# Block-sparse attention and a squared-ReLU MLP on one core: the static value products as one 128-wide stationary operand instead of two of 64

## The chip, the core and the metric

The kernel runs on one core of a Trainium2 chip. A core has a matrix engine (TensorE, PE in the profile) with its own row for loading the stationary operand (PEld), a vector engine (DVE), an activation engine (ACT), a general engine (POOL) and a queue for DMA issues (SP). Matrix products take a stationary operand, which is loaded into the array first, and a moving operand, which then streams past it; the result goes to PSUM banks, everything else lies in SBUF. The metric is the device time of one execution in microseconds (us); the time before is the median of three runs.

## The reference

The attention has 4 batches, 8 heads, 768 positions and 64 values per head. Every block of 32 queries sees its neighbours, the first and the last block, and three sampled blocks; the first and last block of queries see all. The MLP follows on 3072 tokens, with 512 inputs and 2048 hidden units.

```python
mask = |blk_i - blk_j| <= 1, or blk_i or blk_j first or last, or kb in sampled_blocks[qb]
scores = where(mask, q @ k.T / sqrt(64), -1e9)
attn = softmax(scores)
x = attn @ v                               # (4, 8, 768, 64) -> (3072, 512)
h = x @ w_in                               # (3072, 2048)
g = s * relu(h) ** 2 + b
out = g @ w_out                            # (3072, 512), float32
```

## The kernel before, in words

The work has two stages. First comes the attention. It is cut into 52 slots: 40 slots of kind `s` (128 interior queries, four heads each), 4 of kind `h` and 8 of kind `d` for the first and last blocks of queries. For an `s` slot the matrix engine does, in this order: the transposes of the softmax numerators of the slot (`t<-ident,ptile`, line 787; three chunks of 128 keys for each of four heads), the transposes of the result of the slot before (`xs<-ident,xss`, line 858), the scores of the slot after next against its 256 static keys (line 710, or line 724 for the other kinds) and against its sampled keys (line 736), and then the value products of this slot: `av_static` over the two chunks of 128 static keys (line 832) and `av_sampled` over the 96 sampled keys (line 846). Between these, DVE takes the row maxima (line 751), ACT the exponentials (line 763), and both evacuate the transposes to the tiles `pt` (lines 791 and 793). The second stage is the MLP, in products of float32 split into a high and a low part (lines 401 to 403 and 440 to 442), whose last half is done by a seven-product scheme (line 1193).

The order on each engine in the attention and the first part of the MLP is not written by hand: a planner (`Plan.order`) takes operations with costs and priorities and issues each when it could start. One call of `av_static` is one operation of cost 260 in that plan, and that number is the same in both kernels. The matrix engine's own order inside the attention is a fixed line, slot after slot.

`xs` is a PSUM bank of 128 partitions, one per query; `pt[:, c, :]` has 128 keys in its partitions and 128 queries in its columns, and is the stationary operand; `vt[:, c, hp * D:(hp + 1) * D]` has the same keys and the 64 values of one head, and is the moving operand. `halves` are the two slices 0 to 63 and 64 to 127 (of the queries here). The four heads of a slot (`j`) times two chunks (`c`) times two halves make 16 products. The profile counts a float32 product as two records of the stationary load and two of the product, so a slot has 32 of each. A transpose is one record.

Of the kernel before, what the change touches and what calls it, by code (L numbers as in the profile page):

```python
# [202 lines left out]
def kernel(  # L203
# [16 lines left out]
    nc = tc.nc  # L220
# [3 lines left out]
    D = 64  # L224
# [234 lines left out]
    with ExitStack() as es:  # L459
# [240 lines left out]
        halves = [slice(par * D, (par + 1) * D) for par in range(2)]  # L700
# [101 lines left out]
        def out_of(i, j):  # L802
            if i not in xs_of:
                o = bank(NBANK, f"xs{i}")
                nu = 2 if slots[i][0] == "d" else 4
                xs_of[i] = o[:, :nu * D].rearrange("p (h d) -> p h d", h=nu)
                tr_of[i] = o[:, 2 * P:2 * P + nu * D].rearrange("p (a q) -> p a q", q=P)
            return xs_of[i][:, j, :]
# [3 lines left out]
        def av_static(i, j):  # L812
            kind, b, t, x = slots[i]
            n = unit_of[i]
            xs = out_of(i, j)
            if kind == "d":
                vt, pt = vst[(i, j)], pts_of.pop(n + j)
                for c in range(NCH):
                    for par in range(2):
                        rows = halves[par]  # L820
                        nc.tensor.matmul(xs[rows], pt[c // 3][:, c % 3, rows], vt[:, c, rows], start=(c == 0), stop=(c == NCH - 1))  # L821
                return
            vt, pt = vst[(i, 0)], pts_of[n + j][0]
            if kind == "h":
                for par in range(2):
                    nc.tensor.matmul(xs[halves[par]], pt[:, 1, halves[par]], vt[:, (2 * j + par) * D:(2 * j + par + 1) * D],
                                     start=(j == 0), stop=False, skip_group_check=True)
                return
            hp = 2 * (j % 2) + j // 2
            for c in range(2):  # L830
                for rows in halves:
                    nc.tensor.matmul(xs[rows], pt[:, c, rows], vt[:, c, hp * D:(hp + 1) * D], start=(j == 0 and c == 0),  # L832
                                     stop=False, skip_group_check=True)

        def av_sampled(i):
            kind, b, t, x = slots[i]
# [121 lines left out]
        for i, (kind, b, t, x) in enumerate(slots):  # L958
# [52 lines left out]
            for j in range(nu):  # L1011
                pr = j if kind == "d" else 0
                o = op("p", cost[3], u, lambda i=i, j=j: av_static(i, j), cols=col[3], deps=[*evs[j], lv[pr]],
                       alloc=[] if j else [("o", i)], use=[("v", (i, pr)), *(("pt", (u + j, g)) for g in range(ng))] + ([("o", i)] if j else []))
                a_ops.append(o)
# [368 lines left out]
```

## Time and profile before

| | us |
|---|---|
| median of three runs | 809.02 (808.52 to 810.49) |
| profiled execution, its own time | 807.75 |
| span of the instructions in it | 805.9 |
| PE busy in the span | 785.6 (97%) |
| PEld busy | 681.6 (85%) |
| DVE busy | 565.8 (70%) |
| ACT busy | 492.8 (61%) |
| line 832, products, busy | 46.3 (1280 records) |

The profiled execution is 1.27 us below the median. A record of a product reaches from its start to its modelled end, and consecutive records overlap, so the distance between two starts tells more than the length of one. In the timeline a row gives the start, the time from the first start to the last end, the engine and line, the tiles as out<-in, the part of the array as rows*columns, the shape of the operand, and the number of records. In the rows of groups, the numbers behind the bar are busy time and the mean length of one record in ns.

### The profile page before, as it was taken

Reading aid. Unit: us, or ns where it says so; the run is one execution under the profiler, and the core shown is the slowest. Engines: PE = TensorE matmul, PEld = TensorE weight load, DVE = VectorE, ACT = ScalarE, POOL = GpSimd, SP = SyncE. Lnnn points to the kernel's source line nnn. Section 1 sums busy time; section 2 is a strip of 40 time slices with the busy share of each in tenths; the row PEclk is TensorE's granted clock in tenths of the full one; section 3 lists DMA queues with packets and bytes.
Section 4 is the critical chain, followed back from the end, with each engine's and each line's share of the span. In section 5 each row is a group of like instructions: output and inputs, shape, how many; then the busy total and the mean of one; then the engine's idle time right before and its main releaser. Section 6 shows DMA issues by size and latency. Waiting matters only on the chain.

```text
span 805.9 us, 21894 instructions
## 1 busy us (share of the span) xinstructions
PE 785.6 (97%) x8400; PEld 681.6 (85%) x8400; DVE 565.8 (70%) x1445; ACT 492.8 (61%) x1175; POOL 140.9 (17%) x372
## 2 busy tenths in 40 slices
PE   7899998999999999999999999999999999999997
PEld 5588886888887889999899999998889988999996
DVE  5577776888887998999743333388768769766662
ACT  3577776787887787777763333457445457544542
POOL 5422142222400000000000000002223222322321
PEclk8899999999999999999999999999999999999999
DMA  9999798876777533334221010412200012000002
GB/s 252 248 228 325 223 255 247 242 213 206 210 211 248 145 107 108 107 125 131 86 99 39 27 40 27 149 45 88 86 1 7 0 40 90 10 0 1 1 1 78
DMA packets 86071, 95.60 MB, mean 119 GB/s; under 512 B 11344, under 2 KB 64976, under 8 KB 85968
## 3 DMA queue, kind: packets, MB, share of 16 engines
q1 hardware_dynamic: 85968, 94.21, 39.0%
q8 instruction: 66, 1.08, 0.6%
q14 instruction: 37, 0.30, 0.1%
HBM read 77.41 MB, written 12.58 MB: 112 GB/s over the span
## 4 chain that ended last, share of the span: by engine, by line
PE 87%; DVE 5%; DMA 4%; ACT 2%; SPq 1%; issue 1%; DVEq 0%; ACTq 0%
PE m L1193 14%; PE o L441 10%; PE o L442 10%; PE o L440 10%; PE t L787 9%; PE s L710 5%; PE xs L832 5%; PE h L403 5%; PE h L401 5%; PE h L402 5%; PE xs L846 3%; PE s L736 3%; DMA kt<-in_k_seq_dram 2%; PE s L724 1%; PE xs L858 1%; PE xs L821 1%
## 5 line engine op out<-in xcount | busy, mean ns | idle before, releaser
L419 POOL TENSOR_TENSOR hid<-hid,hid 128x384 fp32r<-128x384 f32 x64 | 68.9, 1077 | 512.5 <-ACT hid L1211 510.4
L763 ACT ACTIVATE ptile<-ptile,nm 128x352 f32<-128x352 f32 (+2 forms) x208 | 121.1, 584 | 35.8 <-DVE nm L751 35.5
L1210 ACT ACTIVATE hid<-hid,sb_b,sb_s 128x384 f32<-128x384 f32 x64 | 45.4, 709 | 110.6 <-DVE hid L1204 110.6
L751 DVE CUSTOM_DVE_ANT_0 ptile<-s,ms 128x352 f32<-128x352 f32 x160 | 74.3, 521 | 30.1 <-PE s L736 29.9
L670 POOL COPY kg<-kt 128x128 f32 x264 | 63.9, 302 | 135.1 <-PE s L736 122.6
L401 PE MATMUL h<-x,win 128*128 128x384 f32 x256 | 86.4, 337 | 0.0
L403 PE MATMUL h<-x,win 128*128 128x384 f32 x256 | 86.3, 337 | 0.0
L402 PE MATMUL h<-x,win 128*128 128x384 f32 x256 | 85.9, 336 | 0.0
L787 PE MATMUL t<-ident,ptile 128*128 128x128 f32 x608 | 80.2, 281 | 1.8 <-ACT ptile L763 1.3
L410 DVE SCALAR_TENSOR_TENSOR hid<-hid,sb_s 128x384 f32<-128x384 f32 x64 | 39.4, 616 | 53.9 <-ACT hid L406 53.7
L441 PE MATMUL o<-wout,hid 128*128 128x512 f32 x192 | 76.0, 396 | 0.6 <-DVE wout L85 0.6
L442 PE MATMUL o<-woutr,hid 128*128 128x512 f32 x192 | 75.9, 395 | 0.0
L442 PE MATMUL o<-wout,hid 128*128 128x512 f32 x192 | 75.9, 395 | 0.0
L441 PE MATMUL o<-woutr,hid 128*128 128x512 f32 x192 | 75.8, 395 | 0.0
L440 PE MATMUL o<-wout,hid 128*128 128x512 f32 x192 | 74.8, 390 | 0.0
L440 PE MATMUL o<-woutr,hid 128*128 128x512 f32 x192 | 74.6, 389 | 0.0
L787 PEld LDWEIGHTS t<-ident,ptile 128*128 128x128 f32 x608 | 66.6, 142 | 8.7 <-issue 2.2
L406 ACT ACTIVATE hid<-h 128x384 f32<-128x384 f32 x64 | 31.4, 491 | 69.6 <-PE h L403 69.1
L791 DVE COPY pt<-t 128x384 f32<-128x384 f32 (+1 forms) x104 | 56.3, 543 | 8.3 <-PE t L787 6.6
L419 DVE TENSOR_TENSOR hid<-hid,hid 128x384 fp32r<-128x384 f32 x64 | 35.6, 556 | 34.3 <-ACT hid L415 34.1
L1193 PE MATMUL m<-xT,wop 128*128 128x384 f32 x288 | 58.5, 337 | 0.7 <-DVE sum L1286 0.7
L793 ACT COPY pt<-t 128x384 f32<-128x384 f32 (+1 forms) x104 | 48.1, 474 | 15.3 <-PE t L787 15.2
(169 smaller groups left out, 1660.1 us busy)
## 6 DMA issues: line engine op xcount, KB each, us to landing
vg<-in_v_dram SPq DMA_DIRECT2D x136, 128.0 KB, 3.6
v<-in_v_sta_dram SPq DMA_DIRECT2D x40, 256.0 KB, 4.2
kt<-in_k_seq_dram SPq DMA_DIRECT2D x16, 544.0 KB, 8.0
raw_i<-in_w_in_dram SPq DMA_DIRECT2D x16, 512.0 KB, 4.4
raw_o<-in_w_out_dram SPq DMA_DIRECT2D x16, 512.0 KB, 3.2
v<-in_v_dram SPq DMA_DIRECT2D x16, 384.0 KB, 5.0
xd<-xst SPq DMA_DIRECT2D x44, 128.0 KB, 3.7
out_dram<-ob SPq DMA_DIRECT2D x20, 256.0 KB, 2.4
```

The source lines that it names most:

```text
L401: nc.tensor.matmul(ph, wh, xh, start=(c == 0), stop=False)
L402: nc.tensor.matmul(ph, wh, xl, start=False, stop=False)
L403: nc.tensor.matmul(ph, wl, xh, start=False, stop=(c == NCC - 1))
L419: (eng or nc.vector).tensor_tensor(out=htile(5 + i % 3), in0=t, in1=gh.bitcast(F32), op=ALU.subtract)
L440: nc.tensor.matmul(acc, gh[:, tsl], wout(f, 0), start=first, stop=False)
L441: nc.tensor.matmul(acc, gh[:, tsl], wout(f, 1), start=False, stop=False)
L442: nc.tensor.matmul(acc, gl[:, tsl], wout(f, 0), start=False, stop=last)
L670: nc.gpsimd.tensor_copy(kg[:, m], kts[b][:, :, bass.ds(box["js"][m], BLK)])
L751: nc.vector.tensor_tensor_reduce(out=pt[:, :w], in0=sps.pop((n, g))[:, :w], in1=msk, scale=-scale, scalar=FMAX if g == 0 else nm[:, 0:1], ...
L763: nc.scalar.activation(pt[:, :w], pt[:, :w], AF.Exp, bias=nms[n][:, last:last + 1], scale=-1.0, accum_out=dns[i][:, g, j:j + 1])
L787: nc.tensor.transpose(tp[:, c, :], src[:, c * P:(c + 1) * P], ident)
L1193: nc.tensor.matmul(to, w_, x_, start=(c == 0 and k == 0), stop=(c == 1 and k == 2))
```

## The change

The loop over the two halves of the queries goes. One product takes all 128 columns of `pt` as its stationary operand and writes all 128 partitions of `xs`. The products, the flags of accumulation, the moving operand and the result stay; a slot of kind `s` has eight products instead of sixteen. The other kinds of slot keep their halves.

```diff
             hp = 2 * (j % 2) + j // 2
             for c in range(2):
-                for rows in halves:
-                    nc.tensor.matmul(xs[rows], pt[:, c, rows], vt[:, c, hp * D:(hp + 1) * D], start=(j == 0 and c == 0),
-                                     stop=False, skip_group_check=True)
+                nc.tensor.matmul(xs, pt[:, c, :], vt[:, c, hp * D:(hp + 1) * D], start=(j == 0 and c == 0), stop=False, skip_group_check=True)
```

The matrix engine's order of one `s` slot before, from the last sampled scores to the first sampled value product; the shape is that of the output, and x4 is two chunks times two halves of one head:

```order
L736 MATMUL s_1512<-kg_1_651,qr_1s 32x96 x4
L832 MATMUL xs_1537<-v_0_1031,pt_0_1492 64x64 x4
L832 MATMUL xs_1537<-v_0_1031,pt_0_1497 64x64 x4
L832 MATMUL xs_1537<-v_0_1031,pt_0_1505 64x64 x4
L832 MATMUL xs_1537<-v_0_1031,pt_0_1514 64x64 x4
L846 MATMUL xs_1537<-vg_1_746,pt_0_1492 32x64 x4
```

The same place on the matrix engine now, where the numbers in the tiles' names and the lines behind the edit have shifted:

```order
L736 MATMUL s_1480<-kg_1_651,qr_1s 32x96 x4
L831 MATMUL xs_1505<-v_0_1023,pt_0_1460 128x64 x2
L831 MATMUL xs_1505<-v_0_1023,pt_0_1465 128x64 x2
L831 MATMUL xs_1505<-v_0_1023,pt_0_1473 128x64 x2
L831 MATMUL xs_1505<-v_0_1023,pt_0_1482 128x64 x2
L844 MATMUL xs_1505<-vg_1_746,pt_0_1460 32x64 x4
```

Nothing moves: each group of four products of 64 queries has become a group of two with 128, in the same place. That is so for 160 groups, four in each of the 40 slots; all other rows of the matrix engine, and all rows of DVE, ACT, POOL and SP, follow in the same order as before.

## The prediction

> **What bounds the kernel now.** I read the page first, then the stretches of the attention, then one slot of the timeline. The page:
>
> ```profile
> span 805.9 us, 21894 instructions
> PE 785.6 (97%) x8400; PEld 681.6 (85%) x8400; DVE 565.8 (70%) x1445; ACT 492.8 (61%) x1175; POOL 140.9 (17%) x372
> PE 87%; DVE 5%; DMA 4%; ACT 2%; SPq 1%; issue 1%; DVEq 0%; ACTq 0%
> ```
>
> PE makes up 87% of the chain that ended last. A share of the whole says little about one stage, so the stage with line 832 comes by itself. The columns are busy time and records of PE, PEld, DVE, ACT, POOL, then the granted clock, the DMA share and GB/s:
>
> ```profile
> 46.90:135.00 88.10, 87.50 (x2140) 71.90 (x2132) 65.69 (x242) 65.87 (x201) 26.19 (x108) 1.00 0.89 258
> 150.00:235.00 85.00, 85.00 (x2080) 69.83 (x2074) 72.56 (x255) 68.95 (x209) 20.44 (x84) 1.00 0.75 216
> ```
>
> From 150 to 235 us PE has no idle time at all. One slot, as PE does it:
>
> ```profile
> 199.76 1.53 PE L787 MATMUL t<-ident,ptile 128*128 128x128 f32 x12
> 201.13 0.38 PE L858 MATMUL xs<-ident,xss 128*128 128x128 f32 x2
> 201.44 1.13 PE L710 MATMUL s<-kt,qr_2s 64*128 64x256 f32 x8
> 202.51 0.56 PE L736 MATMUL s<-kg,qr_2s 64*32 64x96 f32 x32
> 203.00 1.15 PE L832 MATMUL xs<-v,pt 128*64 128x64 f32 x32
> 204.08 0.65 PE L846 MATMUL xs<-vg,pt 96*32 96x64 f32 x32
> 204.66 0.33 PE L787 MATMUL t<-ident,ptile 128*128 128x128 f32 x1
> ```
>
> A slot takes 204.66 - 199.76 = 4.90 us, six pieces that follow each other without a gap. So any time that the piece of line 832, 204.08 - 203.00 = 1.08 us, wins or loses goes to the end of the attention, and the MLP, which is PE-bound too, starts that much earlier or later. There are 1280/32 = 40 such pieces.
>
> **What sets the 1.08 us.** The number of records does not. Here are the groups of line 832, and the loads of other lines to compare (busy us, mean ns of one):
>
> ```profile
> L832 PE MATMUL xs<-v,pt 128*64 128x64 f32 x1280 | 46.3, 225 | 0.4 <-issue 0.4
> L832 PEld LDWEIGHTS xs<-v,pt 128*64 128x64 f32 x1280 | 40.6, 138 | 7.2 <-ACT ptile L763 0.6 <-ACT pt L793 0.6 <-issue 0.5
> L846 PEld LDWEIGHTS xs<-vg,pt 96*32 96x32 f32 (+1 forms) x1408 | 22.2, 110 | 6.5 <-DMA vg<-in_v_dram 2.6 <-issue 0.8
> L710 PEld LDWEIGHTS s<-kt,qr_1s 64*128 64x128 f32 x64 | 5.5, 186 | 1.7 <-issue 1.3
> L401 PEld LDWEIGHTS h<-x,win 128*128 128x128 f32 x256 | 48.1, 188 | 2.6
> L787 PEld LDWEIGHTS t<-ident,ptile 128*128 128x128 f32 x608 | 66.6, 142 | 8.7 <-issue 2.2 <-ACT ptile L763 2.1
> ```
>
> A load of 32 columns lasts 110 ns, of 64 columns 138, of 128 columns 186 or 188: about a fixed 80 ns, and on top of it some 28 ns for every 32 columns. The number of rows doesn't count (64 in line 710, 128 in line 401). Only the transposes load 128 columns in 142 ns. How far apart such loads follow each other is read from short windows at the start of a piece, each on the row of the loads or of the products (start, us from the first start to the last end, number of records):
>
> ```profile
> 203.00 0.28 PE L832 MATMUL xs<-v,pt 128*64 128x64 f32 x2
> 203.00 0.14 PEld L832 LDWEIGHTS xs<-v,pt 128*64 128x64 f32 x2
> 203.00 0.20 PEld L832 LDWEIGHTS xs<-v,pt 128*64 128x64 f32 x4
> 203.16 0.87 PE L832 MATMUL xs<-v,pt 128*64 128x64 f32 x24
> 201.44 0.19 PEld L710 LDWEIGHTS s<-kt,qr_2s 64*128 64x128 f32 x2 [0.17 <-issue]
> 201.44 0.30 PEld L710 LDWEIGHTS s<-kt,qr_2s 64*128 64x128 f32 x4 [0.17 <-issue]
> 5.93 2.98 PEld L895 LDWEIGHTS warm<-ident 128*128 128x128 f32 x26
> 199.93 1.36 PE L787 MATMUL t<-ident,ptile 128*128 128x128 f32 x11
> 199.76 0.20 PEld L787 LDWEIGHTS t<-ident,ptile 128*128 128x128 f32 x2
> ```
>
> Line 832's records come in pairs, one for each half of the queries. Two loads together last 0.14 us where one lasts 0.138, two products 0.28 where the first lasts 0.27 (0.22 later on): the halves start within 0.01 us of each other and load and stream side by side, in two halves of the array. The next pair of loads begins 0.20 - 0.14 = 0.06 us later. In the steady part 24 records are 12 pairs, (0.87 - 0.22 - 0.01)/11, or 0.058 us a pair. So the 64-wide version already does both halves in the time of one.
>
> **The change part by part.** It removes one record of each pair, on PE and on PEld: 640 of each. It makes the remaining 16 loads of a slot 128 columns wide instead of 64, and 16 products that use the whole array. The moving operand is the same 64 values, so a product streams no longer than before; what may grow is the load. No row of before has a 128-column load under a 64-value product, so I take the nearest rows:
>
> - From below, the transposes: a load of 128 columns, the next one (0.20 - 0.14) = 0.06 us later. That is line 832's own step today, and the piece would stay at 1.08 us: 0 us.
> - The first two pairs of line 710 load 128 columns of float32 without being transposes, 0.30 - 0.19 = 0.11 us apart, with nothing ahead of them to wait for but the load itself.
> - The warm-up products load 128 columns on the whole array, 26 loads in 2.98 us at full clock: (2.98 - 0.19)/25 = 0.112 us each. Their moving operand has 128 columns, which line 787 streams at (1.36 - 0.27)/10 = 0.109 us. The 0.112 is thus a load hidden under a stream of nearly the same length; a load and a stream one after the other would need 0.22.
> - From above, load and product in turn with no overlap: 0.112 + 0.058 = 0.17 us a step.
>
> I take 0.112: same array, same 128 rows and 128 columns, float32, two records for each product, no transpose. The stream of some 0.06 us hides under it. Then a piece changes by its first load, which nothing hides (0.11 - 0.06 = 0.05 us more), and by 15 steps of 0.112 - 0.058 = 0.054: 0.05 + 0.81 = 0.86 us, from 1.08 to 1.94. Forty pieces make **+34.2 us**. By line 710's 0.11 it would be 0.05 + 0.78 = 0.83, or +33.2.
>
> The semaphore waits at the head of the four groups stay one for each `pt`; those tiles will be ready longer before, since DVE and ACT do the same work in a slot of 5.76 us instead of 4.90 (they are busy 72.56 and 68.95 of 85 us today). No DMA is added or removed.
>
> **What comes back.** PE waits a little inside the attention. Where the cause does not stand on PE's own progress, a slower PE waits less:
>
> ```profile
> 136.04 0.27 PE L846 MATMUL xs<-vg,pt 96*32 96x64 f32 x2 [0.72 <-DMA vg<-in_v_dram]
> 138.82 0.97 PE L846 MATMUL xs<-vg,pt 96*32 96x64 f32 x26 [2.50 <-DMA vg<-in_v_dram]
> 139.72 2.77 PE L787 MATMUL t<-ident,ptile 128*128 128x128 f32 x12
> 139.72:142.33 2.61, 2.61 (x13) 2.61 (x13) 1.30 (x3) 0.48 (x1) 0.00 (x0) 0.50 0.78 224
> 240.88 5.93 DMA raw_i<-in_w_in_dram
> 247.00:250.40 3.40, 2.14 (x17) 1.48 (x17) 3.37 (x14) 2.32 (x8) 0.00 (x0) 1.00 1.05 357
> ```
>
> At 135 us PE waits 0.72 + 2.50 us for gathered values. Their buffer was set free by an earlier slot, so the wait shrinks by the growth of the one changed piece that lies between: 0.86. Behind it the clock was 0.50 and twelve transposes took 2.77 us instead of 1.53; if the shorter wait leaves the clock alone, another 1.2 us; I count half, 0.6. At 247 us PE loses 3.40 - 2.14 = 1.26 us, because DVE (busy 3.37) stood behind a weight transfer that began at 240.88; one changed piece lies between, 0.86 less. Together 2.3 us come back; the bounds are 0 and 0.72 + 2.50 + 1.2 + 1.26 = 5.7. The MLP's rows are untouched.
>
> Sum against the profiled execution: 807.75 + 34.2 - 2.3 = 839.65. It lies 1.27 under the median, so the median becomes **840.9 us** (+3.9%). With the bounds of both terms: 807.75 + 33.2 - 5.7 + 1.27 = 836.5 up to 807.75 + 34.2 + 1.27 = 843.2.
>
> **The rivals.**
>
> *The wide load is as quick as a transpose's (no change).* The mechanism would be that a full-width load is only slow where it shares the array. Place: the 15 steps of the piece. Price: step 0.06 against 0.058, so 0 to 40 x 15 x 0.002 = 1.2 us; 809 to 810. It decides if a 128-column load follows the last within 0.06 us. For it speaks line 787's 142 ns on the same 128x128 shape; against it line 401's 188 ns and the warm-up's 0.112, on that shape too. Trainium skill, "TensorEngine Tiling (Array Packing)", section "Restrictions and Gotchas", says that column tiling shuts out the fast weight load, which would speak for this rival; "TensorE: Matmul & The Clock Gate", section "Weight-path perf modes — Fast Weight Load (FWL) and DoubleRow", keeps that fast load to types other than FP32, and the rows of lines 401, 710 and 832 agree with the latter.
>
> *Fewer records save time (faster).* If each record costs PE a fixed time and the loads are hidden, the second one of each pair, at most 0.01 us behind the first, falls away: 640 x 0.01 = 6.4 us at most, 802.6. It decides only if the load stays under 0.058 us. Against it: both halves run inside one step today. The Trainium skill, "TensorEngine Tiling (Array Packing)", section "Instruction Overhead", gives each matmul an overhead of about 60 cycles; an estimate from it, at the 2.4 GHz of the same notes, is 640 x 25 ns = 16 us less. By that rule two records could not fit well into a step of 58 ns, and the rows of pairs within 0.01 us speak against paying it twice.
>
> *Load and stream in turn (far slower).* Step 0.17: 0.05 + 15 x 0.112 = 1.73 us a piece, +69 us, 878. The warm-up row speaks against it.
>
> *The clock falls* because PE streams only half of the time in the wide piece. A halved window of 3.4 us loses 1.7; one for every slot would be 68 us on top, 909. Against it: the stretch 247 to 250.40, with PE busy 2.14 of 3.40 us, kept 1.00.
>
> **How the numbers follow.** The forecast gets 0.84, no change 0.07, faster 0.03, load and stream in turn 0.03, a falling clock 0.03. Slower by over 0.3% (2.4 us, about what a measurement here can tell from no change) is 0.84 + 0.03 + 0.03 = 0.90; within it 0.07; faster 0.03. The range reaches from 833 to 847: the bounds above, with some 3.5 us on either side for waits that move in the MLP's start, where DVE's decoding of weights stands next to PE. It leaves the rivals out, with 0.16.
>
> **What would show it.** Right: a piece of the changed line takes some 1.9 us, its loads last about 187 ns and follow each other by 0.11 us, a slot takes 5.76 us, and the attention ends some 32 us later with the MLP's length unchanged. The prediction is wrong if the loads of the changed line last 140 ns, or if the piece stays near 1.1 us; if the piece is 1.9 us but the end moves by much less than 30 us, the sum was right and the part that comes back was not.

## The result and the profile after

The changed kernel takes 833.71 us (833.23 to 835.23, six runs) where the kernel before takes 809.23: a ratio of 1.0305, 95% interval 1.0291 to 1.0318. It is slower by some 24.5 us; the predicted 840.9 us was 7.2 too long. Its profiled execution took 833.92 us, 26.2 more than that of before. The page of the changed kernel begins:

```profile
span 832.0 us, 20614 instructions
PE 815.2 (98%) x7760; PEld 714.0 (86%) x7760; DVE 567.5 (68%) x1445; ACT 492.8 (59%) x1175; POOL 141.0 (17%) x372
PE 88%; DVE 4%; DMA 3%; ACT 2%; SPq 1%; issue 1%; DVEq 0%; ACTq 0%
```

PE has 640 records fewer and is busy 29.6 us longer. One slot in the timeline of the changed kernel (line 831 is the changed one):

```profile
149.34 1.53 PE L787 MATMUL t<-ident,ptile 128*128 128x128 f32 x12
150.71 0.38 PE L856 MATMUL xs<-ident,xss 128*128 128x128 f32 x2
151.02 1.13 PE L710 MATMUL s<-kt,qr_4s 64*128 64x256 f32 x8
152.09 0.56 PE L736 MATMUL s<-kg,qr_4s 64*32 64x96 f32 x32
152.58 2.00 PE L831 MATMUL xs<-v,pt 128*128 128x64 f32 x16
154.50 0.65 PE L844 MATMUL xs<-vg,pt 96*32 96x64 f32 x32
155.09 1.53 PE L787 MATMUL t<-ident,ptile 128*128 128x128 f32 x12
```

The slot takes 155.09 - 149.34 = 5.75 us, where it took 4.90; all of the growth is in the fifth row, whose piece now lasts 154.50 - 152.58 = 1.92 us instead of 1.08. Half the records take nearly twice as long. The groups of the changed line, and its loads in a window that begins with a piece:

```profile
L831 PEld LDWEIGHTS xs<-v,pt 128*128 128x128 f32 x640 | 74.4, 191 | 6.7 <-ACT pt L793 0.6
L831 PE MATMUL xs<-v,pt 128*128 128x64 f32 x640 | 79.9, 278 | 0.0
158.32 1.75 PEld L831 LDWEIGHTS xs<-v,pt 128*128 128x128 f32 x15
```

A load lasts 191 ns instead of 138, and the loads follow each other by (1.75 - 0.19)/14 = 0.111 us. The two stretches of the attention that the prediction shows, now (columns as there):

```profile
46.90:135.00 88.10, 88.10 (x1614) 75.52 (x1618) 55.96 (x203) 56.01 (x173) 22.33 (x93) 1.00 0.82 239
150.00:235.00 85.00, 85.00 (x1544) 72.63 (x1543) 62.62 (x216) 58.43 (x175) 22.85 (x94) 1.00 0.67 191
```

PE has no idle time in either, and the granted clock is 1.00. Counted slot by slot in the trace, each of the 40 pieces is 0.85 us longer than its undisturbed length before, 33.9 in sum; the first piece begins 0.4 later; and 8.1 us of waits of before are gone. That makes the 26.2: the first product of the MLP starts at 302.98 instead of 276.80, and what follows it is as long as before.

### The profile page after: what moved, and what is told of

It reads as the page before. It is cut to its first block, busy times and chain, and to the rows that moved or that the text cites. A ratio compares the mean times of both kernels' runs of the same rounds, so it can differ in the third digit from the quotient of the medians.

```text
span 832.0 us, 20614 instructions
## 1 busy us (share of the span) xinstructions
PE 815.2 (98%) x7760; PEld 714.0 (86%) x7760; DVE 567.5 (68%) x1445; ACT 492.8 (59%) x1175; POOL 141.0 (17%) x372
## 4 chain that ended last, share of the span: by engine, by line
PE 88%; DVE 4%; DMA 3%; ACT 2%; SPq 1%; issue 1%; DVEq 0%; ACTq 0%
PE m L1191 13%; PE o L441 10%; PE o L442 10%; PE o L440 10%; PE xs L831 9%; PE t L787 8%; PE s L710 5%; PE h L403 4%; PE h L401 4%; PE h L402 4%; PE xs L844 3%; PE s L736 3%; DMA kt<-in_k_seq_dram 2%; PE xs L856 1%; PE s L724 1%; PE xs L821 1%
## 5 line engine op out<-in xcount | busy, mean ns | idle before, releaser
L831 PEld LDWEIGHTS xs<-v,pt 128*128 128x128 f32 x640 | 74.4, 191 | 6.7 <-ACT pt L793 0.6
L831 PE MATMUL xs<-v,pt 128*128 128x64 f32 x640 | 79.9, 278 | 0.0
```

The costliest lines, as they stand in the source:

```text
L831: nc.tensor.matmul(xs, pt[:, c, :], vt[:, c, hp * D:(hp + 1) * D], start=(j == 0 and c == 0), stop=False, skip_group_check=True)
```

## The experiments

**Is it the load or the stream?** The changed kernel again, with twice the moving columns: the values of two heads, whose results add up in `xs`, so that this run computes something else.

```diff
+            j0, h0 = min(j, 2), min(hp, 2)
             for c in range(2):
-                nc.tensor.matmul(xs, pt[:, c, :], vt[:, c, hp * D:(hp + 1) * D], start=(j == 0 and c == 0), ...)
+                nc.tensor.matmul(xs_of[i][:, j0:j0 + 2, :], pt[:, c, :], vt[:, c, h0 * D:(h0 + 2) * D], start=(j == 0 and c == 0), ...)
```

> The changed kernel with a moving operand of 128 columns (the values of two heads, the results of both added up in xs, so the output is not the reference's): same loads, twice the streaming. Theory (a step is the load of 128 columns, 0.112 us, under which a stream of 0.107 hides): the piece stays within 0.1 us of its 1.93, time within 4 us of the changed kernel's 833.7. Rival (load and stream in turn, the step of 0.112 being a shorter load plus the stream of 0.053): step 0.165, the piece grows by 0.85 us, 34 us more, 868.

Measured: 836.88 us. The timeline of this run:

```profile
154.35 2.05 PE L832 MATMUL xs<-v,pt 128*128 128x128 f32 x16
156.33 0.65 PE L845 MATMUL xs<-vg,pt 96*32 96x64 f32 x32
```

The piece lasts 1.98 us, 0.06 more than with 64 moving columns: the last stream, which nothing follows. Fifteen streams of twice the length cost nothing, so the stationary load sets the step and the stream hides under it. Load and stream in turn is out.

**Does a change of width cost anything by itself?** One chunk wide, the other in halves, in turn:

```diff
             for c in range(2):
-                for rows in halves:
+                for rows in [slice(0, P)] if c == 0 else halves:
```

> One of the two chunks of static keys with the 128-wide operand, the other in halves, in turn for each head: 8 wide and 8 paired steps in a piece and 7 changes between the two. Without a price for a change the piece takes about 8 x 0.112 + 8 x 0.058 + 0.15 = 1.5 us, halfway between before and changed, and the time is some 817 us. If each change costs what the ends of a piece show (last start to next line's start 0.151 instead of 0.058, and a first step longer by 0.05): 7 x 0.14 = 1.0 us more, 2.5 in all, some 857 us.

Measured: 855.7 us, the slowest of all, though one of its two chunks is done in the quick halves. Its timeline:

```profile
154.44 2.59 PE L832 MATMUL xs<-v,pt 128*128 128x64 f32 x24
156.96 0.26 PE L846 MATMUL xs<-vg,pt 96*32 96x64 f32 x4
```

The piece lasts 2.52 us against the 1.5 that the steps alone make. The 1.0 us between them, over seven changes, is the 0.14 for each that the ends of a piece had shown. So PE pays when the array is cut differently, apart from what it loads. What fills these 0.14 us the trace does not tell.

**Where did the waits go?** The prediction gave back 2.3 us, the trace 8.1. The changed operand in the 16 slots ahead of the wait at 135 us alone, then in the other 24 alone:

```diff
+            nth = sum(sl[0] == "s" for sl in slots[:i])
             for c in range(2):
-                for rows in halves:
+                for rows in [slice(0, P)] if nth < 16 else halves:      # the second run: nth >= 16
```

> The 128-wide operand only in the first 16 slots of kind s, all of which end before the wait for gathered values at 135 us. Pieces: 16 x 0.85 = 13.5 us more in every theory. Theory (the queue of DMA issues ran behind PE there, and slower slots ahead of it let it catch up): the wait of 3.2 us and the halved clock behind it vanish although nothing between the freed buffer and the wait is changed; the stretch after slot 17's static piece falls from 9.17 to 3.9 us. Span some 7 us longer than before, 813. Rival (my prediction's step: the wait is tied to the freed buffer and shrinks only by pieces that lie between): it stays at 3.2 us, and the span is 12 to 13 us longer, 818. The wait at 247 us stays in both.

> The 128-wide operand only in the last 24 slots of kind s; the first of them is the one that waits for gathered values at 135 us. Pieces: 24 x 0.85 = 20.3 us more. Theory (the queue catches up over the slots ahead): the wait at 135 us loses about 0.85 us, by the one piece that lies ahead of it, and 2.4 us stay; the wait at 247 us goes. Span 17 to 18 us longer than before, 823. Rival: the wait goes altogether through that one piece, with the halved clock behind it; span 13 us longer, 819.

Measured: 815.14 us and a span of 813.3 for the first, 830.53 and 828.6 for the second. The same slot in the timeline of both, first the run with 16 wide slots, where the static values of this slot are in halves:

```profile
144.92 1.15 PE L833 MATMUL xs<-v,pt 128*64 128x64 f32 x32
146.00 0.65 PE L847 MATMUL xs<-vg,pt 96*32 96x64 f32 x32
```

and the run with the last 24 wide:

```profile
137.78 2.00 PE L833 MATMUL xs<-v,pt 128*128 128x64 f32 x16
139.70 0.58 PE L847 MATMUL xs<-vg,pt 96*32 96x64 f32 x6
143.75 0.86 PE L847 MATMUL xs<-vg,pt 96*32 96x64 f32 x26 [3.46 <-DMA vg<-in_v_dram]
```

In the first, line 847 runs through without a wait, though nothing between the freed buffer and this place differs from before. In the second the wait is as long as ever, though the piece in front of it is 0.85 us longer. Slower slots ahead of it, not the piece next to it, take it away. Both runs held surprises as well: the wait at 247 us went in the first too, which I had expected to stay (the trace has the same slot 1.7 us shorter, without a wide piece near it), and the second was 5.6 us slower than its theory, since the wait lost nothing and, in its 64-wide part, PE waited 2.3 us in three stretches put down to issue (the profile's word for idle time in which it finds nothing that the engine waits for) and 1.1 us for a load of static values. That the first met its 813 us is partly luck: beside the 1.7 us at 247 us, its first piece began 1.4 us earlier than before, and waits put down to issue, 2.2 us by the profile, stood against that.

**Do slower slots do it, whatever slows them?** The kernel before, with the scores of most slots streaming 512 columns instead of 256:

```diff
-                    nc.tensor.matmul(sp[:, :SC], qr[halves[par], 2 * x + k, :], kt[halves[par], 2 * x + k, 192 * t:192 * t + SC],
+                    w = 512 if t < 4 else SC
+                    nc.tensor.matmul(sp[:, :w], qr[halves[par], 2 * x + k, :], kt[halves[par], 2 * x + k, 192 * t:192 * t + w],
```

> The kernel before, 64-wide as it was, with the same longer scores: 0.85 us more in each of 32 slots, 27.3 in sum, from another place than the static values. Theory (any slower slot lets the queue of DMA issues and the weight transfers catch up): the waits at 135 and at 247 us go, with the halved clock, 7 to 8 us back; span 805.9 + 27.3 - 7.5 = 825.7, time 827.5. Rival (they went because the wide static products themselves or their fewer instructions made room): the waits stay, span 833, time 835.

Measured: 827.45 us, span 825.6, as the theory had it. The longer scores and the 64-wide values in its timeline, then the slot that waited before, the last load of gathered values for it, and all of its PE waits on `vg` or issue:

```profile
166.68 1.99 PE L711 MATMUL s<-kt,qr_0s 64*128 64x512 f32 x8
169.08 1.15 PE L833 MATMUL xs<-v,pt 128*64 128x64 f32 x32
146.46 0.31 PE L847 MATMUL xs<-vg,pt 96*32 96x64 f32 x6
148.05 0.61 PE L847 MATMUL xs<-vg,pt 96*32 96x64 f32 x26 [1.28 <-issue]
148.59 1.53 PE L788 MATMUL t<-ident,ptile 128*128 128x128 f32 x12
144.12 0.36 SPq L653 DMA_DIRECT2D vg<-in_v_dram  x1
PE xs L847 <- issue: 1.3, 1, 1.3
```

The wait for the gathered values falls from 3.2 to 1.3 us without any wide product, the twelve transposes behind it take 1.53 us again and not 2.77, and the slot at 247 us is 1.7 us shorter, as in the changed kernel. The profile puts the 1.3 us down to issue, but they are what is left of the wait: in the trace the load of 144.12 landed at 147.96, 0.09 us before PE went on, which is the distance in the run with the last 24 wide too (143.66 and 143.75), while the last packet of instructions (see the quarters below) had landed at 143.07, 5.0 us before. The queue began these loads at 135.93, 1.9 us behind the last read of the buffer (133.36 + 0.65 = 134.01), where it was 5.5 us behind in the kernel before and is 0.8 in the changed one (both worked out further down). So here slower slots bring most of the time back, without wide products and without fewer instructions; that the wait goes altogether did not come true, and the span met the theory because the 0.7 us that this slot keeps were made up at smaller places.

**Four quarters instead of two halves.** If the load sets the step, a narrower one should be quicker still:

```diff
             for c in range(2):
-                for rows in halves:
-                    nc.tensor.matmul(xs[rows], pt[:, c, rows], vt[:, c, hp * D:(hp + 1) * D], start=(j == 0 and c == 0),
-                                     stop=False, skip_group_check=True)
+                for r in range(4):
+                    rows = slice(r * BLK, (r + 1) * BLK)
+                    nc.tensor.matmul(xs[rows], pt[:, c, rows], vt[:, c, hp * D:(hp + 1) * D], start=(j == 0 and c == 0),
+                                     stop=False, tile_position=(0, r * BLK), skip_group_check=True)
```

> The static values with a 32-wide stationary operand: 32 products in a slot instead of 16, four side by side. Theory (the step is the longer of load and stream; a 32-wide load takes some 0.028 us, so the stream of 0.056 bounds): the loads last 110 ns, four products start within 0.02 us, the step falls from 0.058 to 0.056, and since the sampled products that follow are 32 wide too, no changeover lies between. Static and sampled together take 1.48 us instead of 1.67, 0.19 less in each of 40 slots: 7.6 us less on PE, of which the waits at 135 and 247 us may take back up to half. 801 to 806 us. Without the gain at the changeover only the step and the first load count: 0.07 a slot, 2.8 us less. Rival (the number of records costs): 1280 more records at 0.0066 us, 8 us more, 817.

Measured: 833.68 us (827.46 to 835.77), a ratio of 1.0294, interval 1.0255 to 1.0334: not faster but slower, and by more than the rival of a price for each record had it. A slot of this run, and its waits (waited for: us in total, times, longest):

```profile
104.56 1.10 PE L833 MATMUL xs<-v,pt 128*32 128x64 f32 x64
105.48 0.63 PE L847 MATMUL xs<-vg,pt 96*32 96x64 f32 x32
106.05 1.53 PE L787 MATMUL t<-ident,ptile 128*128 128x128 f32 x12
PE t L787 <- issue: 9.7, 3, 4.5
PE xs L847 <- issue: 6.4, 7, 2.0
PE xs L833 <- issue: 4.1, 7, 1.3
PE s L736 <- issue: 1.4, 3, 0.9
q8 instruction: 76, 1.25, 0.7%
```

Where nothing disturbs them, the static and sampled values do what the theory said: they take 106.05 - 104.56 = 1.49 us, where it was 1.67. But PE stands for 21.6 us in 20 places in which no other engine holds it up. Nine of these ends, beside the last landing of a 16 KB packet of the instruction queue in the trace:

```
packet landed  53.75  69.70  75.15  82.93  93.63 162.14 167.74 221.06 269.63
PE went on     55.32  70.97  76.62  84.22  95.06 163.68 169.25 222.52 271.04
```

Each time PE goes on 1.3 to 1.6 us behind a packet; over all 20 places it is 1.1 to 1.8. The page of this run counts 76 such packets, that of before 66, that of the changed kernel 61. Ten packets for 2560 instructions more, five for 1280 fewer, make 256 instructions a packet. So PE waits for its instructions here. The 21.6 us are two thirds of the distance between the theory and this trace, whose span is 24.7 us longer instead of 7.6 shorter. The first piece began 1.7 us later than before; the rest was not worked out.

**Is it the rate of instructions?** Quarters together with the long scores, which add 0.85 us to most slots and no instruction:

> The 32-wide static values again, and the static scores of the slots with t below 4 stream 512 columns instead of 256 (the surplus lands in a free part of the bank and is written over or never read): 0.85 us more PE time in each of 32 slots, with no instruction added. Theory (the idle stretches of the 32-wide run end when a 16 KB packet of instructions has landed; it asks for more instructions in a microsecond than the fetch brings): with 0.85 us more in a slot the fetch keeps up, the idle time put down to issue falls from 21.6 us to under 6 (left in the slots with t = 4), and static plus sampled values take 1.48 us. Span 806 - 7.6 + 27.3 - 7.5 = 818 to 824. Rival (the idle time belongs to four narrow products side by side, whatever the rate): it stays near 20 us, span 845 to 855.

Measured: 841.04 us, span 839.2, between the two. Its waits:

```profile
PE t L788 <- issue: 6.0, 3, 2.1
PE xs L848 <- issue: 2.3, 3, 1.4
PE xs L834 <- issue: 1.0, 3, 0.5
PE s L737 <- issue: 0.4, 1, 0.4
PE xs L848 <- DMA vg<-in_v_dram: 3.4, 1, 3.4
```

The time for issue falls from 21.6 to 9.7 us with the same products, so it hangs on how many instructions a microsecond asks for, and not on the width alone. That rests on one trace of each. The fetch does not keep up, though the theory had said it would, and the wait for `vg` stays at 3.4 us, although most slots ahead of it are slower than before: slower slots do not take that wait away in every case. Why not here, and what delays a packet, was not tested.

**A few wide slots, where PE would wait anyhow.** If slower slots remove the wait at 135 us, four of them might do, and one ahead of the wait at 247 us (`nth` as above):

```diff
-                for rows in halves:
+                for rows in [slice(0, P)] if nth in (12, 13, 14, 15, 35) else halves:
```

> The 128-wide operand in five slots alone: the four that stand ahead of the wait for gathered values at 135 us, and the one ahead of the wait at 247 us. It costs 5 x 0.85 = 4.2 us on PE. Theory (slower slots let the queue of DMA issues catch up, and four slots are enough): the waits give back up to 5.25 + 0.44 + 1.68 = 7.4 us, so the span is some 3 us shorter than before, 806; faster than both kernels. Rival (the queue lags over many more slots than four, so the wait at 135 us stays): only 1.7 to 2.1 us come back, 2 to 3 us slower than before.

Measured: 808.74 us, ratio 0.9996, interval 0.9974 to 1.0018: the same. In its trace the slots with the two waits, and two smaller ones ahead of the first, are 6.0 us shorter outside the wide pieces, which cost 4.2, so some 1.8 us were won there. But PE stood elsewhere:

```profile
PE t L787 <- issue: 1.7, 1, 1.7
PE xs L833 <- issue: 1.6, 2, 0.9
PE xs L847 <- issue: 1.4, 2, 0.9
```

These are 4.7 us, where the profile of before has 0.6. Of them 0.9 us, ended at 138.94, are the rest of the wait for gathered values, whose last load landed at 138.85; the other 3.8 end 1.3 to 1.5 us behind a packet of instructions. No version here beats the kernel before.

## Why the prediction was right, and where it was off

- *What bounds the kernel* and *what sets the 1.08 us*: right. PE is without idle time in both stretches of the attention in the changed kernel too, and that the two halves loaded and streamed side by side fits the quarters, whose 64 records, four to a step, took 105.48 - 104.56 = 0.92 us.
- *I take 0.112*: right, and so the largest term: 0.86 us a piece and 34.2 in sum were forecast (forty times 0.86 would be 34.4), 0.85 and 33.9 measured. The rule that the Trainium skill gives in "TensorE: Matmul & The Clock Gate", section "LDWEIGHTS (loading the stationary operand)", columns over 1.2 in ns, makes an estimate of 107 ns for 128 columns; the trace shows 111 from load to load, and 191 for one load from start to end.
- The rivals: no change, load and stream in turn and a falling clock did not come. The clock stood at 1.00 in both stretches of the attention. That fewer records save time is not so as that rival put it, for the piece grew; but records do cost in another way, through the fetch of instructions.
- *What comes back* failed. The step was "Their buffer was set free by an earlier slot, so the wait shrinks by the growth of the one changed piece that lies between: 0.86". It tied the transfers to the freed buffer. The queue of DMA issues tells otherwise. Before, with the last read of that buffer (line 846) and the place that needs the new values:

```profile
121.81 0.65 PE L846 MATMUL xs<-vg,pt 96*32 96x64 f32 x32
125.01 1.25 SPq L500 DMA_DIRECT2D qr_0s<-in_q_dup_dram  x2
126.36 0.56 SPq L514 DMA_DIRECT2D v<-in_v_sta_dram  x1
127.96 1.44 SPq L653 DMA_DIRECT2D vg<-in_v_dram  x3
135.46 0.36 SPq L653 DMA_DIRECT2D vg<-in_v_dram  x1
```

and the changed kernel:

```profile
133.00 1.20 SPq L500 DMA_DIRECT2D qr_0s<-in_q_dup_dram  x2
134.81 0.33 SPq L514 DMA_DIRECT2D v<-in_v_sta_dram  x1
134.71 0.65 PE L844 MATMUL xs<-vg,pt 96*32 96x64 f32 x32
136.19 2.78 SPq L653 DMA_DIRECT2D vg<-in_v_dram  x3
145.46 0.36 SPq L653 DMA_DIRECT2D vg<-in_v_dram  x1
148.66 0.76 PE L844 MATMUL xs<-vg,pt 96*32 96x64 f32 x32
```

  Before, the buffer was free at 121.81 + 0.65 = 122.46, but the queue still had loads of queries and values ahead and began at 127.96, 5.5 us late. In the changed kernel those loads were issued already, and it began at 136.19, 0.8 us behind 135.36. The last issue stood 0.4 us behind the first need before (135.46 against 135.02) and stands 3.2 ahead of it now. So the wait went, but for the 0.1 us by which line 844 is longer here (0.76 instead of 0.65), and the halved clock behind it went too: 5.25 us in that slot; at 247 us 1.7 instead of 0.86 (why that wait goes altogether was not tested); and 1.2 us at three smaller places, among them 0.6 for instructions at 72 us, which I had not counted. Together 8.1, beyond the 5.7 that I had set as the bound.
- The 7.2 us by which the prediction was too long: 5.8 too little given back, 0.3 too much for the pieces, and 1.5 because the changed kernel's profiled execution lay 0.2 above its median, while I had carried over the 1.27 by which that of before lay below; less 0.4 that was lost ahead of the first piece and not forecast.
- That 833.7 lies inside the stated range of 833 to 847 is luck. It lies below the 836.5 that the sum gave at its lowest, and only the 3.5 us that the range adds for waits in the MLP's start take it in; the MLP kept its length, and what moved were the waits in the attention.

## What to carry to other kernels

Compare column tiles by what bounds a step, the longer of the stationary load and the stream, and not by the number of products: with 64 moving columns in float32, two 64-wide loads side by side fit the stream and one 128-wide load does not. Where the matrix engine is the bound and a queue runs behind, a slower engine can let the queue catch up, so a wait on the path is to be read from what the queue did before it and not only from the buffer that it needs. Where a profile finds no releaser and says issue, comparing the end of the wait with the landings of loads and of instruction packets can tell the two apart. And a finer cut of the same work is worth trying only while the instructions can be brought in as fast as it uses them up.

## What the runs showed of the hardware beside that

- Each change of how the array is cut cost about 0.14 us (seven changes, 1.0 us in the mixed piece). Between static and sampled values in quarters there is no change of width, and the pair took 1.49 instead of 1.67 us.
- PE's instructions come in packets of 16 KB, 256 instructions each, on a DMA queue of their own (q8 in the pages). The quarters stood 21.6 us for that, the one trace of the kernel before 0.6 us, and the run with five wide slots 3.8. It may be a part of the spread from 805.9 to 814.9 us between the runs of the kernel before; that was not tested.
